# An attention and gated-MLP kernel on one core: the framework's scheduler orders it with its timeline simulation in place of its default machine model

## The chip, the cores and the metric

One core of one Trainium2 chip runs the whole program. The metric is the device time in microseconds; the kernel before has 1373.64 us as the median of three runs (1370.13 to 1375.04). A profiled execution of it took 1378.83 us, 1377.1 us of which lie between its first and its last instruction. PE is TensorE, DVE is VectorE, ACT is ScalarE, POOL is GpSimd, SP is the queue that issues the DMAs.

## The reference, cut to what matters

```
# q, k, v: 8 batches x 8 heads x 1152 x 64
q_pool = q.reshape(B, H, S // 2, 2, D).mean(axis=3)          # 576 queries a head
scores = scale * matmul(q_pool, k.T)                         # 576 x 1152
attn   = exp(scores - max) / sum(...)
x      = matmul(attn, v), heads side by side                 # 8 x 576 x 512

h    = maximum(x @ w_in, 0)                                  # 512 -> 1024
u, v = h[..., :512], h[..., 512:]
v_n  = (v - mean) / sqrt(var + 1e-6)
v_s  = einsum('ts,bsd->btd', w_spatial, v_n) + b_spatial     # 576 x 576 over positions
out  = (u * v_s) @ w_out                                     # 512 -> 512, float32
```

## The kernel before, in words

Float32 accuracy is had from float16 pairs: every operand is split into a high and a low half and a product is two or three matmuls.

**Attention.** `attention(i)` handles two heads of one batch; there are 32 such steps. A step has 18 main score tiles (128 keys by 512 queries; L506 and L507 write one, `pss`, three buffers) and 18 small ones of 64 queries (the tail, collected in `ptl`). ACT takes the exponential of a score tile (L512, into `pt`), POOL splits two of them at a time (L524, four `pt` buffers), and PE multiplies each of the 18 tiles with the values: twelve matmuls a tile, 216 a step (L428, L432, L435, into `o`). Twenty-seven more work on the tail (L478 to L480). So a score tile goes PE, ACT, POOL, PE.

**Maxima.** The score of step i+1 needs a bound per query first. `maxima(i+1)` runs beside step i: 30 matmuls (24 of L342, 6 of L333) write 27 pieces into the PSUM tile `pm` (two buffers; the first ones also `pw`), DVE reduces each (L348), gathers them (L352), PE transposes the result (L356), DVE splits it (L358, L359) and two small DMAs (L363) put it into the score operand. There is exactly one L356 matmul a step. **The stretch from one L356 to the next is called a block here**, block 0 ends at the first L356, block 18 is the one between the 18th and the 19th.

**Preparation.** `prep(i+2)` loads and splits queries and keys (ACT L132, L302, L304, DVE L138, POOL L292, L305, DMAs L299 to L313); `norm_v` and `split_v` do it for the values.

**Weights.** `load_weights` turns the 64-bit weights into float32 on DVE and ACT: twelve pieces with six DVE instructions each (L149, L151, L153, L155, L159, L161), called the weight conversions here, and then splits them (L135, L138).

**The MLP.** Two batches make a unit; its x is complete after eight steps, so unit n can begin after 8(n+1) steps. On PE a unit has 108 matmuls L582 (H), 144 of L646 (U: 96 of 512 columns and 48 of 128), 224 of L688 and L689 (P: 112 of 512 columns, 112 of 64) and 108 of L731 (Y). H, U and P write the PSUM tile `pw`, two buffers, which after the first maxima nothing but units uses. Between H and U stands the normalisation of nine tiles on DVE and ACT (L618, L623, L624). A P product takes both `pw` buffers and is read out by DVE with L695 and L698. Before Y comes `split(0)`: a scale that passes through a `pm` tile (`scale_of`, L112) and then ACT L135 and DVE L138 over the whole of `u`. The last unit is run after the last step of attention.

**What sets the order.** The Python code runs generators in turn: after each part of an attention step the maxima, the values, `prep` and the weights get a tick (`Pace`), and a unit gets half a step (`MOE_RATE`):

```
for _ in attention(i):
    for r in run:
        if r:
            r.tick()
    credit = min(credit + MOE_RATE, 2.0)
    while credit >= 1 and units:
        credit -= 1
        unit_step()
```

This gives the order in which the program is written down. The framework's scheduler then goes through it with a model of the machine: each engine gets the earliest written instruction that the model holds to be ready, so a later one goes first where the model says that the earlier one still waits. Buffers of a tile name are handed out in written order. What comes out is a fixed queue for each engine, worked off strictly in that order on the chip, but for the semaphores.

## Time and profile before

| | before |
|---|---|
| median of three runs | 1373.64 us |
| profiled execution | 1378.83 us |
| its span | 1377.1 us |
| busy PE / DVE / ACT / POOL | 1222.1 / 967.1 / 970.6 / 847.0 us |
| mean granted TensorE clock | 0.967 |
| moved by DMA | 123.77 MB, 90 GB/s |

A busy PE counts matmuls whose modelled durations overlap in the pipeline; what PE really needs is read from the distance between the starts of matmuls that follow each other without a wait. The other engines' busy times can be read as they are. Idle time of an engine that nobody waits for costs nothing.

### The profile page before, as it was taken

The page shows a single profiled execution, that of the slowest core. Times are in us where ns is not written, and L with a number is a line of the kernel's source. Part 1 is how long each engine was busy: PE and PEld are TensorE (multiplying, and loading weights), DVE is VectorE, ACT ScalarE, POOL GpSimd, SP SyncE. Part 2 cuts the span into 40 slices and gives each one's busy share as a digit, 9 for nine tenths or more (in the row PEclk, how much of TensorE's full clock was granted, in tenths as well). Part 3 has the DMA queues.
Part 4 walks back from the last instruction along what each step waited for, and adds up shares of the span by engine and source line. Part 5 has one row for each costly group of instructions (what it writes and reads, how often), then busy time and mean ns, then how long its engine had stood idle before and what let it go on. Part 6 is the DMA issues. An engine that isn't in the chain of part 4 may idle for free.

```text
span 1377.1 us, 33478 instructions
## 1 busy us (share of the span) xinstructions
PE 1222.1 (89%) x13696; PEld 741.5 (54%) x13696; DVE 967.1 (70%) x2068; ACT 970.6 (70%) x1632; POOL 847.0 (62%) x492
## 2 busy tenths in 40 slices
PE   3677887788998999889998999889998999899998
PEld 1354555555554665556555666555555566556443
DVE  5799889986869767765668766775667866761455
ACT  6777678779966777768776886768776776655333
POOL 3587677878755666657774766667666576655000
PEclk9998899989999999999999999999999999999999
DMA  7533343434333231244332132244331131101002
GB/s 252 166 97 109 94 124 94 128 93 139 113 96 96 79 94 56 62 126 135 96 96 87 51 91 84 74 118 135 104 96 42 47 94 55 28 24 40 8 1 69
DMA packets 56346, 123.77 MB, mean 90 GB/s; under 512 B 8256, under 2 KB 16448, under 8 KB 56192
## 3 DMA queue, kind: packets, MB, share of 16 engines
q1 hardware_dynamic: 56192, 121.63, 29.8%
q8 instruction: 107, 1.75, 0.5%
q14 instruction: 47, 0.39, 0.1%
HBM read 83.56 MB, written 9.44 MB: 68 GB/s over the span
## 4 chain that ended last, share of the span: by engine, by line
PE 47%; DVE 25%; ACT 8%; POOL 7%; DMA 7%; issue 4%; SPq 1%; POOLq 0%; ACTq 0%; DVEq 0%
DVE mt L348 7%; PE pss L507 5%; PE pss L506 5%; PE pw L688 5%; POOL pt L524 4%; PE pm L342 4%; PE pw L731 4%; PE pw L646 3%; PE o L435 3%; PE o L428 3%; PE pw L582 3%; ACT pt L512 3%; DMA kq<-in_qT_dram 3%; PE o L432 3%; DVE vv L138 2%
## 5 line engine op out<-in xcount | busy, mean ns | idle before, releaser
L524 POOL TENSOR_TENSOR pt<-pt 128x1024 f16<-128x1024 f32 x288 | 567.8, 1977 | 265.9 <-ACT pt L512 253.8
L512 ACT ACTIVATE pt<-pss,lnp,esc 128x512 f32<-128x512 f32 x576 | 439.4, 776 | 156.7 <-PE pss L507 148.1
L348 DVE TENSOR_REDUCE mt<-pm 128x1 f32<-128x384 f32 x730 | 395.8, 552 | 139.1 <-PE pm L342 119.2
L435 PE MATMUL o<-vp,pt 128*128 128x65 f16 x2304 | 282.8, 198 | 20.2 <-POOL pt L524 19.9
L428 PE MATMUL o<-vp,pt 128*128 128x65 f16 x2304 | 284.8, 196 | 13.0 <-DVE xm L443 12.8
L506 PE MATMUL pss<-qhi,khi 128*128 128x64 f16 (+1 forms) x1152 | 279.6, 294 | 9.1 <-ACT pt L512 8.0
L432 PE MATMUL o<-vp,pt 128*128 128x64 f16 x2304 | 284.5, 196 | 0.0
L507 PE MATMUL pss<-xq,klo 66*128 66x64 f16 (+1 forms) x1152 | 280.6, 295 | 4.1 <-DMA xq<-mr 4.1
L428 PEld LDWEIGHTS <-pt 128*128 128x128 bf16 x2304 | 222.7, 101 | 85.1 <-DVE xm L443 22.0
L432 PEld LDWEIGHTS <-pt 128*128 128x128 bf16 x2304 | 221.6, 100 | 50.7 <-issue 10.5
L342 PE MATMUL pm<-khi,qhi 128*128 128x384 f16 x652 | 217.9, 335 | 32.6 <-DVE mt L348 27.7
L435 PEld LDWEIGHTS <-pt 128*128 128x128 f16 x2304 | 220.7, 100 | 31.6 <-POOL pt L524 24.8
L507 PEld LDWEIGHTS <-klo 66*128 66x128 f16 x1152 | 99.1, 100 | 48.8 <-issue 17.3
L132 ACT ACTIVATE klo<-kq 128x1152 f16<-128x1152 f32 x64 | 74.6, 1166 | 63.7 <-DMA kq<-in_kT_dram 49.4
L506 PEld LDWEIGHTS <-khi 128*128 128x128 f16 x1152 | 103.5, 100 | 27.9 <-issue 12.2
L342 PEld LDWEIGHTS <-qhi 128*128 128x128 f16 x768 | 76.8, 101 | 66.3 <-issue 28.5
L524 POOL TENSOR_TENSOR ptl<-ptl 128x1152 f16<-128x1152 f32 x32 | 71.1, 2221 | 57.9 <-ACT ptl L520 57.9
L305 POOL TENSOR_TENSOR klo<-kq,khi 128x640 f16<-128x640 f32 x64 | 85.1, 1341 | 20.1 <-ACT khi L304 19.8
L520 ACT ACTIVATE ptl<-pss,lnp,esc 128x256 f32<-128x256 f32 (+1 forms) x128 | 75.6, 591 | 24.8 <-PE pss L507 24.2
L264 POOL TENSOR_TENSOR vp<-vt,vp 128x576 f16<-128x576 f32 x64 | 80.6, 1264 | 20.3 <-ACT vp L262 20.3
L582 PE MATMUL pw<-wi_h,xg 128*128 128x512 f16 x240 | 90.1, 382 | 0.0
L731 PE MATMUL pw<-wo_h,vv 128*128 128x512 f16 x216 | 80.3, 381 | 4.7 <-DVE vv L138 4.7
(177 smaller groups left out, 2394.2 us busy)
## 6 DMA issues: line engine op xcount, KB each, us to landing
vt<-in_v_dram SPq DMA_DIRECT2D x64, 576.0 KB
kq<-in_kT_dram SPq DMA_DIRECT2D x32, 576.0 KB
kq<-in_qT_dram SPq DMA_DIRECT2D x32, 576.0 KB
khi<-khi SPq DMA_DIRECT2D x96, 144.0 KB
out_dram<-row SPq DMA_DIRECT2D x24, 256.0 KB
qhi<-xq SPq DMA_DIRECT2D x64, 72.0 KB
klo<-klo SPq DMA_DIRECT2D x32, 144.0 KB
vv<-in_w_in_dram SPq DMA_DIRECT2D x8, 512.0 KB
```

Of the source, the lines that this page charges most:

```text
L305: nc.gpsimd.tensor_sub(KL[:, 0, a:z], k0[:, a:z], khh[:, 1, a:z])
L342: nc.tensor.matmul(pm[:, :W], lhsT=qhl[:, h, c0 : c0 + P], rhs=khh[:, h, n * NB : (n + 1) * NB, :], start=True, stop=True,)
L348: nc.vector.reduce_max(out=mt[:, t, n : n + 1], in_=pm[:, :W], axis=AX.X)
L428: nc.tensor.matmul(o[:, t], lhsT=top[:, cols], rhs=vp[:, D : D + D1], start=c == 0 and t == 0, stop=False, skip_group_check=True,)
L432: nc.tensor.matmul(o[:, t, 0:D], lhsT=top[:, cols], rhs=vp[:, 0:D], start=False, stop=False, skip_group_check=True)
L435: nc.tensor.matmul(o[:, t], lhsT=rst[:, cols], rhs=vp[:, D : D + D1], start=False, stop=c == NC - 1, skip_group_check=True,)
L506: nc.tensor.matmul(o, lhsT=khh[:, h, c, :], rhs=qhl[:, h, q], start=True, stop=False)
L507: nc.tensor.matmul(o, lhsT=KL[0:KR, h, c, :], rhs=X[0:KR, h, q], start=False, stop=True)
L512: nc.scalar.activation(pt, ps, AF.Exp, bias=lnp, scale=esc)
L524: nc.gpsimd.tensor_sub(t.bitcast(F16)[:, :, 0::2], t, t.bitcast(BF16)[:, :, 1::2])
L582: nc.tensor.matmul(ph, lhsT=xa[:, cc, c0 : c0 + P], rhs=wa[:, cc, DH:DF], start=n == 0, stop=n == 3 * NCC - 1,)
L731: nc.tensor.matmul(py, lhsT=ga[:, fc, c0 : c0 + P], rhs=wa[:, fc, :], start=m == 0, stop=m == end - 1)
```

## The change: another model behind the scheduler

One argument is added where the program is written down:

```
-    with _tile.TileContext(nc) as tc:
+    with _tile.TileContext(nc, schedule_with_timeline_sim=True) as tc:
```

The scheduler asks a timeline simulation, instead of its default model, which instruction is ready when. No instruction is added or removed: PE has 13616 matmuls of the program in both, DVE 864 of L348, SP the same DMAs. The tiles and their numbers of buffers stay. Only the order in each engine's queue differs, and it differs nearly everywhere (51156 lines of difference on PE). Counted in the built programs, the matmuls of the unit between two L356, blocks 18 to 25 (one unit's whole round of eight steps), and the value matmuls V (L428, L432, L435) with them:

| block | before: V, unit | after: V, unit |
|---|---|---|
| 18 | 216, H60 | 216, U132 P70 |
| 19 | 216, H21 U48 | 216, P154 |
| 20 | 216, U87 | 170, none |
| 21 | 216, U9 P96 | 154, none |
| 22 | 216, P112 | 206, none |
| 23 | 216, P16 Y26 | 288, Y108 |
| 24 | 216, Y55 | 202, H44 |
| 25 | 216, Y27 H27 | 276, H64 U12 |

Blocks 26 to 31 repeat this pattern in both, and blocks 10 to 17 nearly do. Behind the last L356 stand 324 V and 670 unit matmuls before (H108, U144, P224, Y194), and 238 V and 596 after (Y120). In blocks 0 to 9 there are 33 H before and 103 after. The weight conversions on DVE, by block from 0 to 8: before 12, 10, 9, 8, 7, 4, 5, 12, 5; after 22, 25, 3, 0, 0, 12, 10, 0, 0.

Three places show it. First PE, a few rows behind the L356 that opens block 20. Before, a unit's U matmuls (L646) stand between a score tile and the values:

```order
L506 LDWEIGHTS khi_116
L506 MATMUL pss<-qhi_119,khi_116 128x512
L507 LDWEIGHTS klo_107
L507 MATMUL pss<-xq_113,klo_107 128x512
L646 LDWEIGHTS wi_h
L646 MATMUL pw<-xg,wi_h 128x512
L646 LDWEIGHTS wi_h
L646 MATMUL pw<-xg,wi_h 128x512
L646 LDWEIGHTS wi_l
L646 MATMUL pw<-xg,wi_l 128x512
L428 LDWEIGHTS pt
L428 MATMUL o<-vp_101,pt 128x65
```

After, the same stretch has maxima (L342), a score tile and values, and nothing of the unit:

```order
L342 LDWEIGHTS qhi_121
L342 MATMUL pm<-khi_118,qhi_121 128x384
L342 LDWEIGHTS qhi_121
L342 MATMUL pm<-khi_118,qhi_121 128x384
L506 LDWEIGHTS khi_117
L506 MATMUL pss<-qhi_120,khi_117 128x512
L507 LDWEIGHTS klo_108
L507 MATMUL pss<-xq_114,klo_108 128x512
L428 LDWEIGHTS pt
L428 MATMUL o<-vp_102,pt 128x65
```

U and P of this unit have moved into blocks 18 and 19; Y begins in block 23 in both. The buffers of `pm`, `pw` and `pss` are first written in the same sequence in both programs. Second, DVE in the normalisation of a unit (L618 and L624; `row` is the normalised tile, `mt` takes the maxima), block 19 before:

```order
L618 TENSOR_SCALAR row<-vv,mv,rs 128x512
L348 TENSOR_REDUCE mt<-pm 128x1
L618 TENSOR_SCALAR row<-vv,mv,rs 128x512
L402 TENSOR_TENSOR xg<-pm,xg 128x512
L624 TENSOR_TENSOR vv<-row,vv 128x512 x2
L348 TENSOR_REDUCE mt<-pm 128x1 x5
L138 SCALAR_TENSOR_TENSOR qhi_121<-kq,qks,xq_115 128x576
L348 TENSOR_REDUCE mt<-pm 128x1
L618 TENSOR_SCALAR row<-vv,mv,rs 128x512
L348 TENSOR_REDUCE mt<-pm 128x1 x2
```

and block 18 after:

```order
L618 TENSOR_SCALAR row<-vv,mv,rs 128x512 x2
L624 TENSOR_TENSOR vv<-row,vv 128x512 x2
L618 TENSOR_SCALAR row<-vv,mv,rs 128x512
L348 TENSOR_REDUCE mt<-pm 128x1 x2
L618 TENSOR_SCALAR row<-vv,mv,rs 128x512
L624 TENSOR_TENSOR vv<-row,vv 128x512
L618 TENSOR_SCALAR row<-vv,mv,rs 128x512
L624 TENSOR_TENSOR vv<-row,vv 128x512
L348 TENSOR_REDUCE mt<-pm 128x1
L618 TENSOR_SCALAR row<-vv,mv,rs 128x512
```

The nine tiles stand a block earlier and closer together. Third, DVE at the start, ahead of the first L352. Before, the maxima stand in long runs:

```order
L348 TENSOR_REDUCE mt<-pw 128x1 x2
L151 TENSOR_SCALAR vv<-vv 128x512
L155 TENSOR_SCALAR vv<-vv 128x512
L348 TENSOR_REDUCE mt<-pw 128x1 x12
L153 SCALAR_TENSOR_TENSOR u<-vv,u 128x512
```

After, the weight conversions are strewn among them:

```order
L348 TENSOR_REDUCE mt<-pm 128x1 x2
L348 TENSOR_REDUCE mt<-pw 128x1 x2
L153 SCALAR_TENSOR_TENSOR u<-vv,u 128x512
L155 TENSOR_SCALAR vv<-vv 128x512
L348 TENSOR_REDUCE mt<-pm 128x1 x2
L348 TENSOR_REDUCE mt<-pw 128x1 x2
L348 TENSOR_REDUCE mt<-pm 128x1
L159 SCALAR_TENSOR_TENSOR vv<-vv 128x512
```

Twice as many of them now come before the step's maxima are complete.

## The prediction, made before the changed kernel had run

> **What bounds the kernel now.** I read the page's first two parts, then the busy times block by block (front: a block runs from one L356 matmul to the next), then the chain of waits for what a matmul costs. The page's row of engines and its clock row:
>
> ```profile
> PE 1222.1 (89%) x13696; PEld 741.5 (54%) x13696; DVE 967.1 (70%) x2068; ACT 970.6 (70%) x1632; POOL 847.0 (62%) x492
> PEclk9998899989999999999999999999999999999999
> ```
>
> PE leads, the others are at 62 to 70%. Busy times of stretches: blocks 0 to 9; blocks 2 to 8 alone; block 9; then each of blocks 18 to 25, one unit's round; blocks 26 to 31; the rest. The borders are starts of L356. The columns are the length, then busy PE, PEld, DVE, ACT and POOL, the clock, DMA:
>
> ```profile
> 0.00:356.00 356.00, 267.25 (x3147) 169.63 (x3147) 292.42 (x568) 273.65 (x473) 253.11 (x153) 0.92 0.43 128
> 73.00:320.40 247.40, 196.06 (x2481) 129.07 (x2482) 219.69 (x403) 188.25 (x318) 188.57 (x104) 0.89 0.35 103
> 320.40:356.00 35.60, 33.35 (x395) 21.52 (x395) 23.07 (x57) 33.47 (x62) 29.64 (x19) 0.95 0.50 153
> 675.60:713.20 37.60, 36.31 (x413) 21.95 (x412) 22.81 (x57) 28.38 (x47) 26.14 (x16) 1.00 0.30 88
> 713.20:760.10 46.90, 40.43 (x422) 23.84 (x420) 35.62 (x87) 30.33 (x51) 28.02 (x16) 0.93 0.24 71
> 760.10:797.10 37.00, 36.48 (x441) 23.21 (x442) 27.50 (x57) 31.52 (x52) 25.68 (x15) 1.00 0.26 74
> 797.10:836.60 39.50, 38.53 (x467) 23.94 (x466) 26.51 (x64) 29.97 (x55) 25.61 (x16) 1.00 0.33 100
> 836.60:875.60 39.00, 38.14 (x466) 23.11 (x465) 27.81 (x64) 26.95 (x48) 25.27 (x15) 1.00 0.29 85
> 875.60:918.50 42.90, 35.36 (x400) 21.12 (x399) 35.06 (x66) 31.02 (x52) 29.47 (x17) 0.96 0.16 41
> 918.50:953.80 35.30, 34.72 (x408) 21.44 (x407) 19.43 (x49) 27.24 (x43) 22.82 (x15) 1.00 0.56 167
> 953.80:992.00 38.20, 35.65 (x416) 22.55 (x415) 22.78 (x48) 28.65 (x51) 25.41 (x15) 1.00 0.41 123
> 992.00:1229.30 237.30, 221.28 (x2594) 135.18 (x2592) 173.73 (x385) 164.16 (x267) 155.48 (x88) 0.99 0.19 54
> 1229.30:1377.10 147.80, 142.73 (x1123) 74.42 (x1122) 57.59 (x138) 61.68 (x105) 24.83 (x13) 1.00 0.09 31
> ```
>
> What PE needs follows from pieces of the chain, in which the matmuls follow each other without a wait (start, length, instruction):
>
> ```profile
> 598.60 0.06 PE pm L478
> ...
> 610.04 0.03 PE o L428
> 610.32 0.16 PE pm L342
> 610.48 0.22 PE pss L506
> 611.08 0.65 PE pw L731 x3
> 612.25 0.03 PE pss L506
> ```
>
> So 0.216 us for 512 columns, 0.16 for a maximum, 0.03 for a value matmul or 64 columns, 0.06 for the tail's. A block's attention: 36 x 0.216 = 7.8, 36 x 0.03 = 1.1, 216 x 0.03 = 6.5, maxima 24 x 0.16 + 6 x 0.14 = 4.7, tail 27 x 0.06 = 1.5, transposes 0.6: **22.2 us**. A unit: H 108 x 0.216 = 23.3; U 96 x 0.216 + 48 x 0.06 = 23.5; P 112 x (0.216 + 0.05) = 29.8; Y 23.3: **100 us**. With the front's counts blocks 18 to 25 of before hold 35.1, 35.2, 35.3, 37.3, 37.1, 30.4, 33.7 and 34.3 us of PE work, 278 in all; they take 316.4. In blocks 18, 20, 21, 22, 24 and 25 PE binds: 226.6 us for 212.8, a factor of 1.065. In 19 and 23 PE waits for DVE (35 us busy, the two fullest): 89.8 us for 65.6, so 24 of the 38 us that PE loses in the round. Blocks 2 to 8 have no unit: 155 us of PE work in 247.4, DVE busy for 89% (it converts weights), 35.3 us a block.
>
> **The change, part by part.** No instruction comes or goes; each term is a matter of who stands beside whom.
>
> *The round of a unit.* By the counts, PE's work in blocks 18 to 25 becomes 53.5, 41.5, 20.8, 20.3, 21.4, 48.6, 31.2 and 40.9 us: again 278. The unit's U and P have run ahead, but Y needs a scale that passes through a `pm` tile, and these are handed out in written order among the maxima; so Y cannot follow, and three blocks are left with attention alone.
>
> Blocks 20 to 22: the trace has no attention block that is rid of both unit and weights. Below it is bounded by POOL, 847.0 / 32 = 26.5 us, above by the 35.3 of blocks 2 to 8. I take 31, the middle, since ACT's whole 970.6 / 32 = 30.3 stands close by: 93 us for three.
>
> Blocks 19, 23, 24, 25: PE binds, at 1.065: 44.2 + 51.8 + 33.2 + 43.6 = 172.8. Block 18 has the nine normalisations, as block 19 before; they cost DVE
>
> ```profile
> L624 DVE TENSOR_TENSOR vv<-row,vv 128x512 f16<-128x512 f32 x36 | 35.5, 1008 | 2.5 <-ACT vv L623 2.3
> L618 DVE TENSOR_SCALAR row<-vv,mv,rs 128x512 f32<-128x512 f32 x36 | 32.7, 922 | 0.3
> ```
>
> 9 x 1.93 = 17.4 us. They held PE up by 46.9 - 35.2 x 1.065 = 9.4 us before; beside 53.5 us of PE work most of that is covered: 57.0 + 1.5 = 58.5. With P the cover of an eviction goes: in before 0.8 to 2.1 us of other PE work stand between two P products, after it is nothing at three places of seven in the round. The next product waits there for L695:
>
> ```profile
> L695 DVE SCALAR_TENSOR_TENSOR row<-pw,r_v,b_bc 128x512 f32<-128x512 f32 (+1 forms) x54 | 27.7, 513 | 23.5 <-PE pw L689 19.2 <-PE pss L689 3.0
> ```
>
> a 512-column one is about 0.8 us, so between 0 (it was in the 1.065) and 3 x 2; I take 3. Sum: 93 + 172.8 + 58.5 + 3 = 327 against 316.4, **+11**; for blocks 10 to 17 the same again, **+11**. Blocks 26 to 31 have no block like 24 and 25: 58.5 + 44.2 + 3 x 30 (no more values to prepare) + 46.2 x 1.065 = 49.2, + 3 = 245 against 237.3, **+8**. Ends for the round: three blocks at 26.5 and heavy ones at 1.03 give 302 (-15); three at 35.3 and heavy ones at 1.10 give 343 (+27).
>
> A rule of the Trainium skill is to be set against the clock row, which falls to 0.89 in blocks 2 to 8 where PE has the least to do. TensorE: Matmul & The Clock Gate, HAM oscillation, states that idle gaps of PE over about 3.4 us bring it back to half clock. The trace agrees in direction (0.89 beside 1.00), but shows no half. At 0.89 the lone blocks need 21 / 0.89 = 24 us of PE, still under 26.5, so the sum stays; half clock is a rival below.
>
> *The start.* Blocks 0 and 1 hold 47 weight conversions in place of 22. One costs between 0.83 and 1.47 us:
>
> ```profile
> L161 DVE TENSOR_TENSOR u<-u,vv 128x512 f32<-128x512 f32 x12 | 17.7, 1474 | 0.1
> L149 DVE TENSOR_SCALAR vv<-vv 128x512 int32<-128x512 int32 x12 | 10.0, 833 | 1.5 <-DMA vv<-in_w_in_dram 1.5
> ```
>
> 25 x 1.15 = 29 us more for DVE ahead of attention that all waits for its maxima. The two blocks took 73.0 us, with DVE busy for 292.4 - 219.7 - 23.1 = 50; so 29 less 23 of slack at best, 29 at worst: **+18**. Blocks 2 to 8 then have 25 instead of 50, but unevenly, and the eight large splits of w_in (L138) fall into block 5: I put 31.5, 31, 31, 46, 35, 31 and 37 (block 8 has H48 and 274 V, 34.3 us of PE work; x 1.065) = 242.5 against 247.4, **-5**. Block 9, with H55 and 317 V, has 37.4 us of it: 40 against 35.6, **+4**. In all **+17**; from 0, if DVE's early work all comes back, to +40.
>
> *The end.* Behind the last L356 PE has 121 us of work in place of 142, since Y of unit 2 is done. Before: 147.8, 6 more than its work. After, the last attention step has no unit work beside it but some H, so PE waits there; 121 + 6 + 7 = 134, **-14** (from -21, if nothing waits, to -5).
>
> Sum: 1378.8 + 11 + 11 + 8 + 17 - 14 = **1412** on the profiled execution's own time, which stands 5.2 above the median; so **1407** is forecast.
>
> **The rivals.**
>
> *The heavy blocks hide DVE, and the lone ones run at POOL's pace.* The other side: 24 of the 38 us lost in a round stood in the two DVE-full blocks, and in the new order DVE's large pieces lie beside 53.5 and 48.6 us of PE work. Then a round is 215.7 x 1.03 + 3 x 26.5 = 302, twice -15, blocks 26 to 31 at 225 are -12, the end -14, the start +17: 1378.8 - 39 = 1340, by the median 1335. It decides at the lone blocks and the factor: at 1.065 throughout, 215.7 x 1.065 = 229.7 leaves (316.4 - 229.7) / 3 = 28.9 us for a lone block to break even. For it: POOL's 26.5. Against: an attention step passes PE, ACT, POOL and PE again through three and four buffers, and ACT's 30.3 is above. 0.17.
>
> *Values too close behind their scores.* PE's work between a pair's second score tile and its first L428 is under 3 us for 24 of 288 pairs before and for 56 after. What must fit in is an exponential and a split,
>
> ```profile
> L512 ACT ACTIVATE pt<-pss,lnp,esc 128x512 f32<-128x512 f32 x576 | 439.4, 776 | 156.7 <-PE pss L507 148.1
> L524 POOL TENSOR_TENSOR pt<-pt 128x1024 f16<-128x1024 f32 x288 | 567.8, 1977 | 265.9 <-ACT pt L512 253.8
> ```
>
> 0.8 + 2.0 + some 0.4 between engines = 3.2; what is missing sums to 19 us before and 68 after. If PE bears it all on top of the forecast: 1407 + 49 = 1456. Against: in lone blocks PE has slack for it. 0.19.
>
> *The clock.* If the lone blocks ran at half clock, PE would need 42 us in each, 11 over the 31: nine of them, 1407 + 99 = 1506. Against: 0.89 was the least seen. 0.02. This is what the rule of the Trainium skill named above would make of it.
>
> *The queues differ but the rates do not.* If the waits that move are all of the hidden kind, such as POOL's 253.8 us behind ACT, the time stays at 1374. 0.07: with PE at 53.5 us of work in a block and 20 in another this needs chance.
>
> **How the numbers follow.** 0.55 for the forecast, 1407. Its terms' ends add up to -96 and +76; they will not fall together, and ACT's 30.3 speaks against the low ones: a third of the way down and half of it up, its own range is 1375 to 1445. Measurement can tell about 0.5% (7 us). Faster by more: the first rival, 0.17, and no more, since the forecast's own range ends at no change. Same: 0.07. Slower: 0.55 + 0.19 + 0.02 = 0.76. The range leaves out the clock, a little above the second rival, and the most of the first: 1362 to 1465.
>
> **What would show it.** In the profile after: the spacing of L356 near 58, 44, 31, 31, 31, 52, 33 and 44 us for blocks 18 to 25; the end after the last L356 near 134; the first two blocks near 93; PE's waits in the lone blocks ended by ACT and POOL. Wrong, if the lone blocks come in under 28.9 (then faster), if heavy blocks exceed 1.10 times their work (then the second rival), or if the clock row falls under 0.8 there.

## The result, and the profile after

The changed kernel takes 1462.07 us as the median of four runs (1456.14 to 1464.8), the kernel before 1371.89 us on the same chip: a ratio of 1.065, with a 95% interval of 1.0609 to 1.0691. The forecast was 1407 in a range from 1362 to 1465. The profiled execution took 1461.7 us, its span is 1459.9.

The page's row of engines and its clock row, after:

```profile
PE 1254.9 (86%) x13696; PEld 749.7 (51%) x13696; DVE 958.3 (66%) x2068; ACT 964.9 (66%) x1632; POOL 833.4 (57%) x492
PEclk9679978899989999999999989999999999999999
```

DVE, ACT and POOL are busy for a little less than before; PE has 13696 matmuls in both. PE is busy for 32.8 us more, and idle for 1459.9 - 1254.9 = 205.0 us in place of 1377.1 - 1222.1 = 155.0, so 50.0 more; together they are the 82.8 us of the span.

The mean granted clock on the page fell from 0.967 to 0.947, but these means overstate the change. Single records of the clock are either 1.00 or 0.50, and they begin only at 58.6 us before and at 30.1 us after; the page counts the time ahead of them as full clock. Matmuls there are as slow as at 0.50, as those of 512 columns show before and after 58.6 us in the kernel before:

```profile
57.79 0.63 PE L507 MATMUL pss<-xq,klo 66*128 66x512 f16 x1
59.83 0.38 PE L506 MATMUL pss<-qhi,khi 128*128 128x512 f16 x1
```

With those starts counted as 0.50, PE is busy at half clock for 104 us before and for 130 after. So some 13 of the 32.8 us are work of the same size at half clock, about 10 of them in blocks 10 to 31 (30 us busy at half clock there before, 50 after). This is an estimate, from the clock's records and PE's busy time.

Busy times of stretches, after, in the columns of the prediction: blocks 0 and 1; 2 to 8; 9; then 18, 19, the three lone blocks 20 to 22 together, 23, 24, 25; 26 to 31; the end:

```profile
0.00:93.40 93.40, 46.23 (x353) 24.36 (x354) 71.68 (x136) 65.14 (x121) 42.78 (x36) 0.78 0.57 181
93.40:342.40 249.00, 205.33 (x2462) 131.60 (x2459) 182.99 (x394) 187.39 (x318) 179.47 (x104) 0.89 0.36 109
342.40:389.30 46.90, 39.95 (x517) 25.67 (x516) 21.13 (x53) 33.52 (x57) 30.43 (x18) 1.00 0.32 96
...
729.90:794.30 64.40, 58.79 (x556) 33.38 (x555) 43.69 (x95) 35.93 (x66) 25.96 (x15) 0.95 0.20 57
794.30:840.70 46.40, 43.10 (x508) 25.88 (x507) 33.95 (x72) 27.42 (x50) 23.70 (x13) 1.00 0.20 59
840.70:936.80 96.10, 76.97 (x943) 49.05 (x943) 65.78 (x139) 71.39 (x117) 71.21 (x42) 0.91 0.30 83
936.80:994.40 57.60, 51.67 (x539) 28.94 (x539) 28.82 (x62) 38.64 (x62) 29.18 (x18) 1.00 0.42 133
994.40:1030.50 36.10, 33.72 (x384) 20.57 (x385) 23.58 (x56) 27.68 (x46) 26.63 (x16) 1.00 0.26 76
1030.50:1078.10 47.60, 43.20 (x503) 26.47 (x500) 27.65 (x65) 30.95 (x51) 28.60 (x17) 1.00 0.29 83
1078.10:1331.10 253.00, 227.29 (x2554) 136.26 (x2553) 167.02 (x361) 158.35 (x258) 148.00 (x84) 0.96 0.19 57
1331.10:1459.90 128.80, 122.71 (x952) 63.98 (x950) 56.67 (x136) 52.94 (x94) 18.87 (x10) 1.00 0.07 24
```

| stretch | before | forecast | after |
|---|---|---|---|
| blocks 0, 1 | 73.0 | 91 | 93.4 |
| blocks 2 to 8 | 247.4 | 242.5 | 249.0 |
| block 9 | 35.6 | 40 | 46.9 |
| blocks 10 to 17 | 319.6 | 331 | 340.6 |
| block 18 | 37.6 | 58.5 | 64.4 |
| blocks 19, 23, 24, 25 | 163.3 | 172.8 | 187.7 |
| blocks 20 to 22 | 115.5 | 93 | 96.1 |
| blocks 26 to 31 | 237.3 | 245 | 253.0 |
| the end | 147.8 | 134 | 128.8 |

The shape is the one forecast: the lone blocks near 31, the end shorter, the first two blocks longer. What differs is the price: every stretch but the end is longer than the forecast, block 9, block 18 and the other heavy ones by most. What PE waits for in the whole kernel is read from the groups of instructions; their columns are total busy us and mean ns, then the idle time ahead and what ended most of it. Before:

```profile
L507 PE MATMUL pss<-xq,klo 66*128 66x64 f16 (+1 forms) x1152 | 280.6, 295 | 4.1 <-DMA xq<-mr 4.1
L506 PE MATMUL pss<-qhi,khi 128*128 128x64 f16 (+1 forms) x1152 | 279.6, 294 | 9.1 <-ACT pt L512 8.0
L435 PE MATMUL o<-vp,pt 128*128 128x65 f16 x2304 | 282.8, 198 | 20.2 <-POOL pt L524 19.9
L342 PE MATMUL pm<-khi,qhi 128*128 128x384 f16 x652 | 217.9, 335 | 32.6 <-DVE mt L348 27.7
```

and after:

```profile
L506 PE MATMUL pss<-qhi,khi 128*128 128x64 f16 (+1 forms) x1152 | 284.2, 297 | 44.2 <-ACT pt L512 36.6
L507 PE MATMUL pss<-xq,klo 66*128 66x64 f16 (+1 forms) x1152 | 279.1, 298 | 14.7 <-DMA xq<-mr 14.7
L435 PE MATMUL o<-vp,pt 128*128 128x65 f16 x2304 | 266.4, 198 | 3.2 <-POOL pt L524 3.2
L342 PE MATMUL pm<-khi,qhi 128*128 128x384 f16 x652 | 208.0, 340 | 51.2 <-DVE mt L348 41.3
```

PE now waits for a free score buffer (L506, until ACT has read one: 36.6 us in place of 8.0), for a free `pm` buffer (L342, until DVE has: 41.3 in place of 27.7), and for the row of maxima that the DMA L363 brings at a step's start (L507, 14.7 in place of 4.1). The wait of the values for the split (L435) has all but gone. In which stretch these waits lie is taken up below.

### The profile page after: what moved, and what is told of

The parts are those of the page before. It is cut to its first block, busy times and chain, and to the rows that moved or that the text cites. A ratio compares the mean times of both kernels' runs of the same rounds, so it can differ in the third digit from the quotient of the medians.

```text
span 1459.9 us, 33497 instructions
## 1 busy us (share of the span) xinstructions
PE 1254.9 (86%) x13696; PEld 749.7 (51%) x13696; DVE 958.3 (66%) x2068; ACT 964.9 (66%) x1632; POOL 833.4 (57%) x492
## 4 chain that ended last, share of the span: by engine, by line
PE 47%; DVE 21%; ACT 14%; DMA 11%; issue 4%; POOL 1%; SPq 1%; ACTq 0%; DVEq 0%; POOLq 0%
DVE mt L348 7%; PE pw L688 6%; DMA vt<-in_v_dram 5%; PE pss L506 5%; PE pss L507 5%; PE pm L342 4%; ACT pt L512 4%; PE pw L582 4%; PE pw L731 3%; PE o L428 3%; PE o L435 3%; PE pw L646 3%; PE o L432 2%; DMA khi<-khi 2%; DMA kq<-in_kT_dram 2%
## 5 line engine op out<-in xcount | busy, mean ns | idle before, releaser
L524 POOL TENSOR_TENSOR pt<-pt 128x1024 f16<-128x1024 f32 x288 | 554.3, 1937 | 355.7 <-ACT pt L512 328.1
L512 ACT ACTIVATE pt<-pss,lnp,esc 128x512 f32<-128x512 f32 x576 | 428.4, 779 | 149.4 <-PE pss L507 95.7
L348 DVE TENSOR_REDUCE mt<-pm 128x1 f32<-128x384 f32 x730 | 386.7, 550 | 191.1 <-PE pm L342 150.6
L506 PE MATMUL pss<-qhi,khi 128*128 128x64 f16 (+1 forms) x1152 | 284.2, 297 | 44.2 <-ACT pt L512 36.6
L507 PE MATMUL pss<-xq,klo 66*128 66x64 f16 (+1 forms) x1152 | 279.1, 298 | 14.7 <-DMA xq<-mr 14.7
L428 PE MATMUL o<-vp,pt 128*128 128x65 f16 x2304 | 272.0, 196 | 2.1 <-DVE xm L443 1.1
L432 PE MATMUL o<-vp,pt 128*128 128x64 f16 x2304 | 271.2, 196 | 0.0
L435 PE MATMUL o<-vp,pt 128*128 128x65 f16 x2304 | 266.4, 198 | 3.2 <-POOL pt L524 3.2
L342 PE MATMUL pm<-khi,qhi 128*128 128x384 f16 x652 | 208.0, 340 | 51.2 <-DVE mt L348 41.3
L428 PEld LDWEIGHTS <-pt 128*128 128x128 bf16 x2304 | 221.2, 101 | 41.0 <-DVE xm L443 7.7
L435 PEld LDWEIGHTS <-pt 128*128 128x128 f16 x2304 | 221.0, 100 | 40.4 <-issue 13.2
L432 PEld LDWEIGHTS <-pt 128*128 128x128 bf16 x2304 | 220.8, 100 | 26.9 <-issue 12.7
L507 PEld LDWEIGHTS <-klo 66*128 66x128 f16 x1152 | 100.7, 101 | 112.1 <-issue 71.5
L506 PEld LDWEIGHTS <-khi 128*128 128x128 f16 x1152 | 105.7, 103 | 63.2 <-issue 35.2
L342 PEld LDWEIGHTS <-qhi 128*128 128x128 f16 x768 | 73.8, 102 | 106.4 <-issue 63.5
L132 ACT ACTIVATE klo<-kq 128x1152 f16<-128x1152 f32 x64 | 74.2, 1159 | 41.0 <-DMA kq<-in_kT_dram 37.9
L305 POOL TENSOR_TENSOR klo<-kq,khi 128x640 f16<-128x640 f32 x64 | 84.9, 1343 | 20.1 <-ACT khi L304 20.0
L524 POOL TENSOR_TENSOR ptl<-ptl 128x1152 f16<-128x1152 f32 x32 | 68.7, 2148 | 31.3 <-ACT ptl L520 31.2
L348 DVE TENSOR_REDUCE mt<-pw 128x1 f32<-128x384 f32 x134 | 70.9, 546 | 16.5 <-PE pw L342 15.4
L646 PE MATMUL pw<-xg,wi_h 128*128 128x512 f16 (+1 forms) x336 | 81.4, 332 | 0.0
```

What stands on the lines that cost most here:

```text
L305: nc.gpsimd.tensor_sub(KL[:, 0, a:z], k0[:, a:z], khh[:, 1, a:z])
L342: nc.tensor.matmul(pm[:, :W], lhsT=qhl[:, h, c0 : c0 + P], rhs=khh[:, h, n * NB : (n + 1) * NB, :], start=True, stop=True,)
L348: nc.vector.reduce_max(out=mt[:, t, n : n + 1], in_=pm[:, :W], axis=AX.X)
L428: nc.tensor.matmul(o[:, t], lhsT=top[:, cols], rhs=vp[:, D : D + D1], start=c == 0 and t == 0, stop=False, skip_group_check=True,)
L432: nc.tensor.matmul(o[:, t, 0:D], lhsT=top[:, cols], rhs=vp[:, 0:D], start=False, stop=False, skip_group_check=True)
L435: nc.tensor.matmul(o[:, t], lhsT=rst[:, cols], rhs=vp[:, D : D + D1], start=False, stop=c == NC - 1, skip_group_check=True,)
```

## The experiments

Theories, as they came up. **A**: the bunching of the unit is what costs, more than the forecast's factor said. **B** (later **E**): the fine order inside a block does, whoever stands there. **D**, from a look at the order: in blocks 9 to 31, but for one, the changed kernel has L356, the last of the next step's maxima, behind all 18 main score tiles of the running step, the kernel before three or four tiles ahead of their end; so the next step's first score stands still until L356, DVE and L363 are through. **F**: it is PE's order, in L356's place and in maxima that follow each other and wait for DVE. **G**: it is the queues of the other engines. All ratios are against the kernel before, run on the same chip. Seven of the eighteen results (`rate10`, `rate06`, `pe_written`, `att_written`, `dveb`, `spb`, `restb`) lie above every time that was expected for them.

### Unit work spread under the new order, bunched under the old

In `spread` every PE instruction of a unit's step is queued behind the score tile written last, so that the units are distributed as in before; `both` does the same for the weight conversions on DVE, behind the last written L348:

```
+        with tc.issue_after(mark["PE"]):
+            done = step(units[0]) is None
...
+            mark["PE"] = nc.tensor.matmul(o, lhsT=KL[0:KR, h, c, :], rhs=X[0:KR, h, q], start=False, stop=True).ins
```

`rate10` and `rate06` keep the default scheduler and bunch the units in the program as written:

```
-    MOE_RATE = 0.5
+    MOE_RATE = 1.0
```

(0.6 in `rate06`.) Expected:

> The timeline order is kept, but each step of a unit queues its PE instructions behind the score tile written last, so that the units cannot run ahead: by the built order blocks 10 to 31 hold 30 to 38 us of PE work each again, and 180 Y stand behind the last maxima in place of 120 (13 us more there). Theory A, the bunched units cost it all: blocks 10 to 31 go back from 942 us to some 873, the end gains 13, so 1462 - 69 + 13 = 1406. Theory B, the fine order of PE costs it (maxima and scores behind DVE and ACT at many places), whatever the units do: blocks 10 to 31 stay above 920, so 1450 or more. In between, the share of each is read from blocks 18 to 25: 316 before, 348 with the change.

> As spread, and the weight conversions are queued on DVE behind the maxima written before them: by the built order blocks 0 to 8 hold 0, 8, 14, 11, 13, 2, 8, 14 and 2 of them in place of 22, 25, 3, 0, 0, 12, 10, 0 and 0. Theory A (the two displaced kinds of work are the loss): the start goes back from 389 to some 356 as well, so 1373. Theory B (fine order): the start stays at 380 or more and the whole above 1430.

> The default scheduler with MOE_RATE 1.0 in place of 0.5: the written order itself bunches the units. By the built order a round of eight blocks has 34, 48, 51, 43 and 36 us of PE work in five blocks and 22 in three, the start and the fine order are those of before, and 108 Y in place of 194 stand at the end (19 us less). Theory A (bunching alone makes heavy blocks take 1.17 times their work): 211 x 1.17 + 3 x 31 = 340 a round, 23 more than before; with 2.7 rounds and the end 1372 + 62 - 19 = 1415. My prediction's factor of 1.065: 318 a round, 1372 + 5 - 19 = 1358. Theory B (fine order, which this kernel does not have): as the latter, 1350 to 1360.

> The default scheduler with MOE_RATE 0.6: the units are spread over seven blocks of eight, and 117 Y in place of 194 stand behind the last maxima. Both theories agree that the end gets 16 us shorter; the round has one block with 24 us of PE work which takes 30 or so, and the others 30 to 41. At a factor of 1.065 for those: within 3 us of before a round, so 1372 - 16 + 6 = 1362; by theory A with a steep price for every us of bunching 1372.

Measured: `spread` 1527.69 us (1.1106, interval 1.1069 to 1.1143), `both` 1532.81 (1.1161, 1.1139 to 1.1182), `rate10` 1456.06 (1.0592, 1.0562 to 1.0621), `rate06` 1407.77 (1.0249, 1.0222 to 1.0276). So theory A alone falls: without the bunching the new order is worse. A part of the 155 us of `spread` is the clock: over its blocks 10 to 31 the mean granted clock is 0.92, before 0.98, and PE is busy for 133 us at 0.50 in place of 30, so by estimate up to 52 of the 123 us by which these blocks are longer are work at half clock. Nor is the bunching by itself a bargain: under the default order it costs nearly as much as the whole change, and a fifth of the rise in the rate already 35 us. Blocks 18, 19, 20 and the three after 21 in `rate10`:

```profile
707.50:769.00 61.50, 52.36 (x491) 29.40 (x490) 45.18 (x98) 38.13 (x64) 26.02 (x16) 0.97 0.19 55
769.00:823.50 54.50, 52.15 (x556) 30.00 (x555) 30.88 (x65) 30.38 (x54) 26.62 (x15) 1.00 0.21 61
823.50:878.50 55.00, 48.47 (x487) 27.21 (x486) 42.01 (x82) 33.92 (x55) 26.18 (x14) 0.94 0.18 51
...
916.80:1012.40 95.60, 80.60 (x1060) 53.71 (x1060) 60.83 (x143) 70.96 (x115) 73.94 (x44) 0.91 0.33 91
```

Block 19 holds 50.6 us of PE work by the counts and takes 54.5, a factor of 1.077, close to the forecast's. Blocks 18 and 20 hold 48.2 and 43.2 and take 61.5 and 55.0, 1.28 and 1.27: there DVE has 42 to 45 us to do, the normalisation and `split(0)`. PE's waits name DVE in both, but are not all of the surplus: in block 18 it stands 6.5 us for L348 to free `pm`, in block 20 2.9 for the split of `u` (L138), 1.4 for L348 and 1.2 for a P product's L695. The lone blocks take 31.9 each, as in the changed kernel.

### The place of L356

`early` is the changed kernel, and `early_spread` the kernel `spread`, with the main score tiles 15 to 17 of a step queued behind L356; `late` and `mr125` are the kernel before with the pace of the maxima changed:

```
+        mark["X"] = nc.tensor.transpose(out=pt[:NT, :P], in_=mx, identity=ident).ins
...
+            with tc.issue_after(mark["X"]) if k >= 15 else nullcontext():
+                main_tile(st["pt"][-1][:, k % 2], c, h)
```

```
-    MAX_RATE = 1.0
+    MAX_RATE = 0.75
```

(1.25 in `mr125`.)

> As the kernel spread (timeline order, units tied to their attention steps), but score tiles 15 to 17 of a step also wait in PE's order behind the transpose L356 of the next step's maxima, so that L356 stands three main tiles ahead of the step's end everywhere (spread has it behind the last tile in blocks 9 to 31; before four tiles ahead). Theory D (the late L356 breaks the score stream at every step's border; the gap on ACT there was 10.0 us a step in spread and 0.7 in before): the gap falls to under 2 us, 23 borders x about 6 to 7 us come back, 1375 to 1415. Rival E (the fine order otherwise, values too close behind scores, queues of the other engines): the time stays over 1480.

> As the changed kernel, but score tiles 15 to 17 wait behind L356 as in early_spread; the units stay bunched. Theory D with the bunching as a cost of its own: the border gap goes (9.4 us to under 2), but in the heavy blocks unit work lay in it, so only the light ones and the half-filled ones gain: 1405 to 1440. D alone, bunching free: 1370 to 1390. Rival E: 1450 to 1465, no change.

> The kernel before (default order) with one number changed: the maxima run at 0.75 in place of 1.0 per turn, so that L356 stands behind the last score tile of the step before in all blocks; units spread as before. Theory D: the border gap comes (0.7 to some 9 us), 23 to 31 borders x 6 to 7 us: 1510 to 1590, about the time of spread. Rival E: 1370 to 1395.

> The kernel before with the maxima at 1.25 per turn: L356 stands seven main tiles ahead of the step's end in place of four, units spread as before. Theory D: the border gap was 0.7 us already, so nothing or a little is won: 1360 to 1375. If earlier maxima compete with the scores for PE and DVE instead, up to 1385.

Measured: `early_spread` 1485.6 us (1.0815, 1.078 to 1.0851), `early` 1456.82 (1.0624, 1.0584 to 1.0665), `late` 1424.92 (1.0378, 1.0348 to 1.0408), `mr125` 1383.08 (1.0075, 1.0056 to 1.0093). The waits of PE in `spread` (the three columns are total us, how often, the longest; its L511 is L507):

```profile
PE pm L342 <- DVE mt L348: 62.6, 87, 2.7
...
PE pss L511 <- DMA xq<-mr: 25.2, 23, 4.4
```

and in `early_spread`:

```profile
PE pm L342 <- DVE mt L348: 78.6, 98, 3.6
...
PE pss L511 <- DMA xq<-mr: 8.2, 6, 4.6
```

The wait for the row of maxima, 23 times in `spread`, 19 of them just behind the borders of blocks 9 to 31, goes from 25.2 to 8.2 us, and 42 us of the time come back, some 30 of them in blocks 10 to 31; D's wait is there. But it is a part: 114 us of `spread`'s 155 stay, the wait for DVE grew, and `early` is no faster than the changed kernel by more than the interval. Nor does L356's place alone bring the wait: `late` has L356 behind the last score in every block and pays 53 us, where D expected 138 or more, but PE waits there for the row of maxima once, 4.1 us, as before; what grew is its wait for `pm`, 42.1 us in place of 27.7. Maxima earlier than before gain nothing (`mr125`).

### Maxima in rows, and PE in the written order

`burst` and `burst_late` are the kernel before, at a `MAX_RATE` of 1.0 and 0.75, with three maxima written in a row and then three turns without one:

```
                 nc.vector.reduce_max(out=mt[:, t, n : n + 1], in_=pm[:, :W], axis=AX.X)
-                yield
+                if n == 2:
+                    yield
+                    yield
+                    yield
```

`pe_written` is the changed kernel with every PE instruction tied behind the PE instruction written before it; in `att_written` those of the units are left out of the chain:

```
+        for ins in list(nc.cur_bb.bb.instructions):
+            if ins.engine == _mybir.EngineType.PE:
+                if prev is not None:
+                    tc.add_manual_dep(
+                        ins, prev.name,
+                        _mybir.DependencyInfo(_mybir.DependencyClass.NoSync, _mybir.DependencyReason.DATA),
+                        reason="written order",
+                    )
+                prev = ins
```

> The changed kernel with one thing taken back: every PE instruction is tied behind the one written before it, so that PE's order is the written one, near that of before (L356 four main tiles ahead of a step's end, 48 of 480 maxima in blocks 10 to 25 within 0.3 us of PE work behind another, before 55, spread 202); the other four engines stay in the timeline's order. Theory F (PE's order is the whole cause: L356 behind the last score, and maxima in runs that wait for DVE's L348): 1360 to 1395. Rival G (a good part lies in the queues of DVE, ACT, POOL and SP): 1410 to 1480.

> As pe_written, but the units' PE instructions are left to the timeline: attention's own PE order is the written one, and the units bunch into three blocks of each eight (60.0, 61.3 and 45.6 us of PE work, the other five 22 us each). This is the forecast's own case, bunching without the other faults. Bunching at the forecast's factor of 1.065, 31 us for a lone block: 178 + 155 = 333 a round, so 1385 to 1425. If bunching itself costs what the kernel rate10 paid: 1445 to 1480.

> The kernel before (default order), its maxima written three in a row and then three turns without one, in place of one a turn; nothing else moves (129 of 480 maxima within 0.3 us of another, before 55, after 150; L356 four tiles ahead as before). Theory F: PE waits for L348's buffers as in spread (29.5 us of waits a round behind mt against 9.8), at half to all of that: 1400 to 1440. Rival G: 1370 to 1385.

> Both of PE's faults put into the kernel before: maxima three in a row, and at 0.75 a turn, so that L356 stands behind the last score (170 of 480 within 0.3 us). Theory F, the two adding: the 1425 of the kernel late and the surplus of burst, 1455 to 1510, most of the way to spread's 1528. Rival G: 1425 to 1440, as late alone.

Measured: `pe_written` 1512.81 us (1.1003, 1.0979 to 1.1026), `att_written` 1546.45 (1.1252, 1.1226 to 1.1278), `burst` 1374.27 (1.0002, 0.9982 to 1.0023), `burst_late` 1436.04 (1.0453, 1.0423 to 1.0484). The scheduler split the rows of three of `burst`: in blocks 10 to 25 PE mostly has two maxima in a row, and the third a score matmul or more later. Theory F falls as the whole cause: maxima in pairs cost nothing where the rest stands as before (some 10 us more where L356 is late too, `burst_late` against `late`), and PE in the written order does not bring the time back. In `att_written`, the forecast's own case, blocks 17, 18, the four lone ones 19 to 22, 23 and 24:

```profile
722.70:791.40 68.70, 64.47 (x552) 35.81 (x550) 40.16 (x95) 42.83 (x75) 32.13 (x19) 0.95 0.19 57
791.40:858.80 67.40, 63.35 (x638) 35.78 (x639) 40.35 (x89) 34.85 (x64) 23.28 (x14) 1.00 0.17 49
858.80:997.30 138.50, 111.48 (x1418) 74.34 (x1419) 79.34 (x196) 97.26 (x156) 97.46 (x58) 0.89 0.33 95
997.30:1054.40 57.10, 50.98 (x463) 28.56 (x462) 30.44 (x59) 34.78 (x55) 26.77 (x15) 0.94 0.30 91
1054.40:1090.90 36.50, 28.11 (x356) 18.45 (x355) 19.67 (x51) 26.94 (x41) 25.19 (x15) 0.91 0.29 90
```

The heavy ones hold 60.0, 61.3 and 45.6 us of PE work by the counts: factors of 1.15, 1.10 and 1.25 where the forecast had 1.065. The lone ones take 34.6 each, and 36.5; the forecast had 31. No other engine is full in any of them. In the whole of `att_written` it is the wait of the values for the split (L435 for L524) that grew most, 56.3 us in place of 19.9, and then that of L506 for L512, 43.0 in place of 8.0; but in blocks 17 and 18 they are only 2.2 and 1.8 us, so they do not explain the heavy blocks.

### One queue after another back to its old order

The order of whole queues is now frozen to that which the kernel before has on the chip, instruction by instruction, and the timeline orders the rest anew around them; what it makes of the rest is not the order of the changed kernel: PE in `peb`, PE and DVE in `pedveb`, PE, DVE and ACT in `pedveactb` (POOL then comes out as before by itself), DVE alone in `dveb`. With all five frozen nothing of the change is left. `ORDER` holds the sequence of each queue:

```
+        queue_in_order(nc, tc, _mybir)
...
+    for engine, text in ORDER.items():
...
+            if prev is not None:
+                tc.add_manual_dep(
+                    ins, prev.name,
+                    mybir.DependencyInfo(mybir.DependencyClass.NoSync, mybir.DependencyReason.DATA),
+                    reason="order",
+                )
+            prev = ins
```

> The changed kernel with PE's order frozen to that of before, instruction by instruction; the timeline orders the other four (DVE 358 instructions, ACT 409, POOL 68, SP's 143 out of their place in before). The kernel pe_written, whose PE order was only near that of before, took 1513. Theory G (the queues of the others): 1470 to 1520. If 1513 came of what was left different in PE's order: 1370 to 1400.

> PE's and DVE's order frozen to those of before; the timeline orders ACT (384 out of place), POOL (67) and SP (136). Theory G1 (DVE's queue: maxima and evictions behind normalisations, conversions and splits): back to 1370 to 1395. Rival G2 (ACT's and POOL's queues, exponentials and splits behind loads' conversions): stays at 1440 to 1510.

> PE, DVE and ACT frozen to before; POOL then comes out as in before too, and only SP's DMA queue differs (98 out of place). G1 or G2: 1368 to 1385. Rival G3 (SP's queue, loads issued early or late): what remains above 1385 is SP's.

> DVE's order alone frozen to that of before; the timeline orders PE (which bunches the units into it as far as DVE's order lets it), ACT, POOL and SP. G1 (DVE alone was the cause in the changed kernel): 1375 to 1410. If PE's own order costs as well: 1420 to 1480.

Measured: `peb` 1456.3 us (1.059, 1.0554 to 1.0625), `pedveb` 1441.74 (1.0492, 1.046 to 1.0524), `pedveactb` 1418.28 (1.0325, 1.0295 to 1.0354), `dveb` 1512.87 (1.0996, 1.0963 to 1.1028). PE's order gives back 6 us (the intervals of the two overlap), DVE's 15, ACT's with POOL's 23, and 44 remain with SP's alone. Those 44 have a place: blocks 10 to 31 of `pedveactb` take 915.9 us in place of 873.3. In these kernels lines stand two higher, L134 is L132, the split of freshly loaded keys. The waits of ACT in `pedveactb`:

```profile
ACT pt L514 <- PE pss L509: 151.3, 161, 3.6
ACT klo L134 <- DMA kq<-in_kT_dram: 98.5, 22, 8.8
```

and in before:

```profile
ACT pt L512 <- PE pss L507: 148.1, 153, 4.0
ACT klo L132 <- DMA kq<-in_kT_dram: 49.4, 20, 4.7
```

ACT stands there for 98.5 - 49.4 = 49 us more, with the exponentials behind it in its queue, and a part of it reaches PE: in blocks 10 to 31 PE waits 24.0 us for L512 to free a score buffer, in place of 1.0. In block 16 ACT stands 8.4 us for keys, and PE 6.9 for ACT. In SP's queue the load of keys L222 now has others ahead of it that wait for something: at the start of block 16 a load of values L229, at which SP stands for 3.6 us, the two L363, and L313, at which it stands for 1.7. It is issued 6.5 us after L356 there, and 1.1 us ahead of L356 before. In the changed kernel itself this is not seen: ACT waits there for the keys for 37.9 us, less than before.

### Do the shares add?

`spb` freezes SP's queue alone, `restb` all but PE's, by the same code.

> SP's DMA order alone frozen to that of before; the timeline orders the rest (units bunched as in the changed kernel). If the shares add (SP's order was worth 44 us when the other four stood as in before): 1410 to 1425. If a share is only worth something once the other queues fit: 1445 to 1470.

> DVE, ACT, POOL and SP frozen to before, only PE's order left to the timeline (which then bunches the units hardly at all, 29.6 to 41.4 us of PE work a block, but runs maxima close: 172 of 480 within 0.3 us). If PE's order is worth only the 6 us that freezing it gave first: 1374 to 1385. If PE's order costs once the others are right: 1395 to 1450.

Measured: `spb` 1504.53 us (1.0919, 1.088 to 1.0958), `restb` 1465.35 (1.0653, 1.0636 to 1.0671). They do not add. A new order of PE alone costs 91 us (`restb`), a new order of the other four alone 82 (`peb`), the change 90. These are not two parts of one order, though: with the rest frozen the timeline makes another PE order (no block of `restb` has more than 41.4 us of PE work, the changed kernel's block 18 has 53.5), and in `peb` blocks 0 and 1 hold 27 and 21 weight conversions in place of 22 and 25. The two kernels pay in different places, as the stretches of `restb` show (blocks 0 and 1, blocks 18 to 25):

```profile
0.00:75.00 75.00, 40.06 (x273) 20.29 (x274) 51.33 (x110) 51.14 (x94) 35.98 (x33) 0.98 0.62 198
...
712.00:1060.60 348.60, 312.48 (x3423) 184.15 (x3422) 218.21 (x488) 230.72 (x390) 210.98 (x121) 0.96 0.29 83
```

and those of `peb`:

```profile
0.00:91.30 91.30, 39.83 (x272) 19.83 (x272) 68.03 (x137) 62.62 (x120) 38.84 (x33) 0.96 0.59 186
...
730.70:1058.20 327.50, 299.12 (x3424) 183.01 (x3423) 218.34 (x487) 234.34 (x390) 206.61 (x120) 0.97 0.30 88
```

| stretch, against before | after | `restb` | `peb` |
|---|---|---|---|
| blocks 0 to 9 (356.0) | +33 | +11 | +40 |
| blocks 10 to 31 (873.3) | +68 | +82 | +39 |
| the end (147.8) | -19 | -7 | 0 |

The start is long where the other queues are new: DVE has 68.0 us of work in the first two blocks in `peb` and 51.3 in `restb`. The rounds are long where PE's order is new: `restb` takes 348.6 us for blocks 18 to 25, the changed kernel 348.2, and in `restb` the units are hardly bunched at all (29.6 to 41.4 us of PE work a block by the counts). The waits of PE in `restb`:

```profile
PE pm L344 <- DVE mt L350: 42.9, 77, 2.6
PE pss L508 <- ACT pt L514: 30.0, 38, 2.7
PE pm L358 <- DVE mx L354: 24.8, 17, 3.2
```

The first two are the two that grew in the changed kernel. As totals of the kernel they do not tell the queues apart, since `peb`, with PE's order of before, has 39.3 and 22.7 us of them. In blocks 10 to 31 they do:

| PE's waits in blocks 10 to 31, us | before | after | `restb` | `peb` | `pedveactb` |
|---|---|---|---|---|---|
| L342 for L348 to free `pm` | 20.1 | 26.3 | 34.1 | 18.3 | 20.8 |
| L506 for L512 to free `pss` | 1.0 | 14.4 | 23.6 | 5.7 | 24.0 |

There the wait for `pm` grows where PE's order is new (`restb`) and not in `peb`; the wait for `pss` grows in `restb`, and with SP's queue alone (`pedveactb`) too. In `restb`'s built order, 172 of the 480 maxima of blocks 10 to 25 have less than 0.3 us of PE work between them and the one ahead, in rows of up to six; in before 55, hardly ever more than two. `pm` has two buffers, and L348 takes 0.55 us for what L342 writes in 0.16. So rows longer than the buffers are a likely cause of that wait; it is not shown, since `burst`, with 129 such maxima in shorter rows, has 34.4 us of it in the whole kernel and lost no time. And both waits together grew by 20 us in the changed kernel's blocks 10 to 31, which are 68 us longer.

## Why the prediction was right in direction and short in size

**Right.** *Direction and range*: slower, and 1462 lies just inside 1362 to 1465, but 55 us above the forecast; the surplus of 90 us is nearly three times the 33 forecast. *The lone blocks*: 96.1 us for the three, 93 forecast, over the 28.9 each that decided against the first rival; the lone blocks of `rate10` (31.9) and `att_written` (34.6) say the same. *The first two blocks*: 93.4 for 91, with DVE 22 us busier in them (71.7; it was 50); `restb`, with the old DVE queue, has 75.0. *The end*: 128.8 for 134. *Block 18 above its work*: 64.4 for 58.5, direction right.

**The step that failed** is "Blocks 19, 23, 24, 25: PE binds, at 1.065". The factor was taken from blocks of before, and the step took it to be a property of a full PE, which would hold for any order in which PE has enough to do. Measured: 187.7 us for 162.2 of work, 1.157, and with block 18 252.1 for 215.7, 1.169. The round's miss of 21 us is this: 14.9 in those four blocks, 5.9 in block 18, 3.1 in the lone ones, less the 3 put down for P's evictions. So the sign set for being wrong, heavy blocks at over 1.10 times their work, came, but not with the cause that was named beside it (see the rivals). The factor belongs to an order: under a new PE order alone (`restb`) the same 278 us of work take 348.6 without bunching, 1.25, where before took 316.4, 1.14. I had counted which work stands in which block, and not how it alternates inside one.

No single wait stands in the factor's place. In blocks 18, 19, 23, 24 and 25 PE takes 36.4 us over its 215.7 of work. 21.6 of them are idle: 9.2 for a free `pm` or `pss` (4.6 of L342 and 1.7 of L333 for L348, 2.9 of L506), 3.1 of Y for its split, 2.6 of values for L524, 2.4 of L356 for L352, the rest in smaller pieces. The other 14.8 are PE being busy for longer than my count, some 3 of it at half clock. In the six bound blocks of before it was 13.8 us over 212.8, 6.8 of them idle. Why PE's waits become so many in these blocks is open. Blocks 10 to 17 (10 us more than forecast) and 26 to 31 (8) repeat the round.

**The start** was too small, 33 for 17: 2.4 in the first two blocks, 6.5 in blocks 2 to 8, 6.9 in block 9. The term counted DVE's conversions alone; `peb` has the old order on PE and is 40 longer there, so PE's order is not needed for it. The frozen queues show two more parts. With DVE's order taken back as well (`pedveb`) the first two blocks go from 91.3 to 77.5 us, as the term had it. With ACT's and POOL's (`pedveactb`) blocks 0 to 9 go from 383.8 to 352.0, below before's 356.0; the term had nothing for these two queues. That the weight conversions, tied back in `both`, bring the first two blocks from `spread`'s 95.7 to 78.9, but make blocks 2 to 9 26 us longer, fits this.

**The rivals.** *Values too close behind their scores* gave 1456, near the result, and is wrong as a mechanism: the wait it speaks of (L435 for L524) fell from 19.9 to 3.2 us. That the number came near is luck. (It did grow in two other kernels with bunched units, to 40.9 us in `rate10` and 56.3 in `att_written`.) *Half clock in the lone blocks* was seen for 17 of their 96.1 us, hence 0.91. The prediction's reading that the trace before shows no half clock was wrong: a mean of 0.89 is made of records of 1.00 and 0.50, and one stretch in block 19 of before reads

```profile
734.50:741.30 6.80, 6.55 (x41) 3.90 (x42) 5.51 (x19) 4.05 (x8) 1.18 (x1) 0.50 0.34 104
```

More work at half clock, some 13 of the 83 us by the estimate above, is a cost that no term of the sum had. *The queues differ but the rates do not* was no better: new queues of the other four cost 82 us with PE's order untouched.

**What stays open.** Bunching under the default order (`rate10`, 1456.06 - 1372.53 = 84 us), a new PE order without bunching (91) and a new order of the other four (82) each cost nearly what the change costs, 90. Why these do not add is not shown; that the timeline makes another order each time is one reason at hand, that a wait on one queue hides a wait on another is a guess. Of the 68 us in blocks 10 to 31, 40 are PE idle and 28.6 PE busy, about 10 of these at half clock; the other 18 or so are not explained. Nor is it shown what in the timeline's model of the machine puts the maxima in rows. No kernel of these beats the one before; `burst` equals it.

## What to carry to other kernels

A ratio of time to work read from one order is not to be used for another: before adding up an engine's load by block, look at how its kinds of work alternate, and how long the rows of one kind are against the number of their buffers (here such rows went with a longer wait; that they caused it is not shown). A scheduler's order is one fit of five queues; taking over one queue from a better order can cost more than it gives (`spb` and `dveb` were 42 and 51 us slower than the changed kernel, with the other queues ordered anew around the frozen one), so compare whole orders. Where a DMA queue is worked off in order, look at which load waits for a buffer ahead of one that somebody needs.

## What the runs showed of the hardware that was not expected

TensorE's clock was seen to halve after pauses of 2.81 and 2.19 us. PE in the changed kernel, in block 18 (start, length, instruction, idle time ahead):

```profile
751.01 0.19 PE L428 MATMUL o<-vp,pt 128*128 128x65 f16 x1
754.01 0.48 PE L342 MATMUL pm<-khi,qhi 128*128 128x384 f16 x1 [2.81 <-DVE mt L348]
...
754.87 0.63 PE L506 MATMUL pss<-qhi,khi 128*128 128x512 f16 x1
755.30 0.63 PE L507 MATMUL pss<-xq,klo 66*128 66x512 f16 x1
755.73 0.63 PE L646 MATMUL pw<-xg,wi_h 128*128 128x512 f16 x1
...
758.97 0.38 PE L506 MATMUL pss<-qhi,khi 128*128 128x512 f16 x1
759.18 0.38 PE L507 MATMUL pss<-xq,klo 66*128 66x512 f16 x1
```

After a pause of 2.81 us, 512 columns go 0.43 us apart for some 3 us, and then 0.21 again, so that by estimate this wait cost about 1.5 us on top of itself. In block 19 of before, a pause of 2.19 us, up to 734.14, was followed by the 6.8 us at 0.50 shown above; a pause of 2.05 us up to 375.83 in the changed kernel was not followed by any. The Trainium skill (TensorE: Matmul & The Clock Gate, HAM oscillation) puts the limit at gaps over about 3.4 us; here 2.81 and 2.19 us were enough.
